# Four bfloat16 sums of halves of x, moved from VectorE to copying and adding transfers

## The chip, the cores and the metric

The kernel runs on one core of a Trainium2 chip. The metric is the device time of one execution in microseconds (us); the time of the kernel before is the median of three runs. The engines are named as the profile names them: PE (TensorE's matmuls) and PEld (its weight loads), DVE (VectorE), ACT (ScalarE), POOL (GpSimd) and SP (SyncE, which here only issues transfers).

## The reference

Two linear-attention blocks, A and B, take the same x of 2048 rows and 640 columns with weights of their own, and a gate mixes their outputs. Everything is bfloat16 outside; there are 32 heads of 20 columns.

```python
qkv = (x @ wqkv) split into q, k, v of 32 heads
phi = lambda t: jnp.where(t > 0, t + 1, jnp.exp(t)) + 1e-6
pq, pk = phi(q), phi(k)
kv = jnp.einsum("bhsd,bhse->bhde", pk, v)
z = jnp.einsum("bhsd->bhd", pk)
o = einsum(pq, kv) / (einsum(pq, z)[..., None] + 1e-6)
block = o.reshape(B, S, D) @ wo
...
g = _sigmoid((x * gate_w).sum(-1, keepdims=True))
return g * a + (1 - g) * b
```

## The kernel before

The kernel never forms v. It computes G = x^T phi(k), a 640 x 640 matrix, for each block, and takes the heads' kv from G and the weights of v afterwards. The 2048 rows of x lie in `xn` as 16 chunks of 128 rows (partitions) with 640 columns each; `xT` holds x transposed; `pk` holds phi(k) like `xn`, `pqT` holds phi(q) transposed.

**Order of the work.** PE's order is written out by hand, and the order of the calls is the order of every engine's instructions. First come the transposes of x and the k chunks of block A (`k_first`, `k_chunk`), with parts of its q. Then the loads of the rest of `xn` (L810), of `wv` and of `wo` (`load_w`, `load_wo`) are issued on SP. In the second part, from L819 on, the last two k chunks of A follow, then `q_pass` (the rest of q of A, L778 to L796), then `g_pass` (column block 4 of G, L447) and `g_strassen` (column blocks 0 to 3 of G, L493). Block B follows with the same two functions after a stage in which its q and k are woven together. At the end come the products with the output weights.

**The product that the change touches.** `g_strassen` computes column blocks 0 to 3 of G with seven block products instead of eight (a Strassen scheme in Winograd's form). x is cut into x11 and x21 (chunks 0 to 7; columns 0 to 255 and 256 to 511) and x12 and x22 (chunks 8 to 15, the same columns). phi(k) is cut into b11 and b12 (chunks 0 to 7; left and right 320 columns) and b21 and b22 (chunks 8 to 15). The scheme needs four sums of halves of x, made once and used by both blocks:

- S1 = x21 + x22 and S2 = S1 - x11, in the tile `S3` (shown as S in the profile)
- S3 = x11 - x21, written over x21 in `xn`
- S4 = x12 - S2, in the first part of the tile `M[1]` (shown as MB in the profile)

Beside them stand four differences of halves of phi(k) for each block: T1 = b12 - b11, T2 = b22 - T1, T3 = b22 - b12, T4 = b21 - T2 (`k_sum`, L474). They lie in `pqT[1]` (pqTB) for block A and in `xT` and a weight tile for block B.

The four sums of x are made by `x_sum` (L464), which issues one DVE instruction each through the helper `add_rows` (L627 is the line that the profile shows). S1 and S2 are called inside the loop at L784, S3 inside the loop at L788, and S4 inside `g_strassen` at L524, behind the fourth difference of phi(k).

PE goes through the products of `g_strassen` in this order: x11 by b11 into the bank `even`; ACT copies that into the bank `odd` (L510). Then S2 by T2 is added into `odd`, x12 by b21 into `even`, S3 by T3 into `odd`, S1 by T1 into a fresh `even`, x22 by T4 into `odd`, S4 by b22 into `even`. DVE combines results with copies u2 and u3 of the banks (L505 through the helper `add`, and L543), ACT copies the others into G (`GT`). Between the products PE also makes the sums for the denominators (`rec_pass`, denA, with DVE's reciprocals at L617 and L622) and spreads the reciprocals (`norm_spread`, exA, L664).

**Queues.** SP issues, in this order around the change: the transposing loads of `xT`, the loads of `xn` (L810), `wvA` (L767), `woA` in two pieces (L773, L774), then `wkB` (which waits until the last k chunk of A has been computed), `g_rows` and `ge` (the gate's row, written to memory and read back spread out, L226 and L229; DVE reads `ge` at L617), and `wqB`. GpSimd issues no transfer in the whole kernel; it makes constants in the first 10 us.

Of the kernel before, what the change touches and what calls it, by code (L numbers as in the profile page):

```python
# [12 lines left out]
ALU = mybir.AluOpType  # L13
# [8 lines left out]
HF = D // 2  # L22
# [10 lines left out]
def kernel(  # L33
# [11 lines left out]
    nc = tc.nc  # L45
# [35 lines left out]
    def ps(name, slot=None):  # L81

        return ps_raw(name, slot).bitcast(FP32).rearrange("p (b n) -> p b n", b=2)
# [27 lines left out]
    SX = {k: S3[:, k - 1] for k in (1, 2)}  # L111
# [47 lines left out]
    for n in range(1, NB):  # L159
        for c in range(DT):  # L160
            nc.sync.dma_start_transpose(
                out=xT[:, c, n * HB:(n + 1) * HB], in_=x2[n * HB:(n + 1) * HB, c * P:(c + 1) * P]
# [4 lines left out]
    for r in range(4):  # L167
# [3 lines left out]
        out=spread[:].rearrange("p (h t) -> p h t", t=TW), in_=I4[:, :, None].to_broadcast([P, H, TW])  # L171
    )
    nc.gpsimd.memset(maskE[:], 1.0)
    for sign, base in ((1, 0), (-1, Dh - 1)):
        nc.gpsimd.affine_select(
            out=maskE[:], in_=maskE[:], pattern=[[-sign * Dh, K6 // Dh], [0, Dh]],
# [3 lines left out]
    for r in range(4):  # L180
        rows = slice(32 * r, 32 * r + 32)
        for sign, base in ((1, 0), (-1, Dh - 1)):
            nc.gpsimd.affine_select(
                out=E4[rows], in_=E4[rows], pattern=[[sign, D]],
# [155 lines left out]
    def q_unit(b, m, h, lifted=False, slot=None, between=None):  # L340

        pt = ps(f"q{'AB'[b]}", slot)
        q_two(b, [(m, 2 * h), (m, 2 * h + 1)], pt)
        phi(pqT[b][:, m, h * 2 * HB:(h + 1) * 2 * HB].rearrange("p (b n) -> p b n", b=2), pt, lifted, between)
# [116 lines left out]
            start=(i == 0), stop=(i == ST - 1),  # L461
        )

    def x_sum(k):  # L464

        x11, x21 = [xn[:, 0:hc, n:n + ic] for n in (0, ic)]
        x12, x22 = [xn[:, hc:ST, n:n + ic] for n in (0, ic)]
        a, b, op = {
            1: (x21, x22, ALU.add), 2: (SX[1], x11, ALU.subtract),
            3: (x11, x21, ALU.subtract), 4: (x12, SX[2], ALU.subtract),  # L470
        }[k]
        add_rows(SX[k], a, b, op)

    def k_sum(b, k):  # L474

        b11, b12 = [pk[:, 0:hc, n * HF:(n + 1) * HF] for n in range(2)]
        b21, b22 = [pk[:, hc:ST, n * HF:(n + 1) * HF] for n in range(2)]
        t = TK[b]
        left, right = {1: lambda: (b12, b11), 2: lambda: (b22, t[1]), 3: lambda: (b22, b12), 4: lambda: (b21, t[2])}[k]()
        add_rows(t[k], left, right, ALU.subtract)  # L480

    def g_prod(pt, left, right, first, between=None):

        for i in range(hc):
            if between is not None and i == hc // 2:
                between()
            for n in range(2):
                nc.tensor.matmul(  # L488
                    pt[:, n, 0:HF], lhsT=left[:, i, n * P:(n + 1) * P], rhs=right[:, i, :],
                    start=(first and i == 0), stop=(i == hc - 1), skip_group_check=not first,  # L490
                )

    def g_strassen(b, select, second, spare):  # L493

        x11, x12 = [xn[:, k:k + hc, 0:ic] for k in (0, hc)]
        x22 = xn[:, hc:ST, ic:2 * ic]
        b11 = pk[:, 0:hc, 0:HF]
        b21, b22 = [pk[:, hc:ST, n * HF:(n + 1) * HF] for n in range(2)]
        lo, hi = GT

        def temp(name):
            return work.tile([P, 2, HF], FP32, tag="osb", name=name, bufs=3)

        def add(dst, pt, sb):
            nc.vector.tensor_tensor(out=dst, in0=pt[:, :, 0:HF], in1=sb[:], op=ALU.add)  # L505

        even, odd = ps("gs0", 0), ps("gs1", second)
        sel = []
        g_prod(even, x11, b11, True, lambda: sel.append(select()))
        nc.scalar.copy(out=odd[:, :, 0:HF], in_=even[:, :, 0:HF])  # L510
        if b == 1:
            for rows in part[1:4]:
                p_diff(rows)
        rts = rec_pass(b, sel[0], 2)
        g_prod(odd, SX[2], TK[b][2], False)
        u2 = temp("u2")
        nc.scalar.copy(out=u2[:], in_=odd[:, :, 0:HF])
        if b == 1:
            k_sum(1, 4)
        g_prod(even, x12, b21, False)  # L520
        nc.scalar.copy(out=lo[:, 0:2, :], in_=even[:, :, 0:HF])
        if b == 0:
            k_sum(0, 4)
            x_sum(4)  # L524
        norm_spread(b, rts, (2, spare))
        g_prod(odd, SX[3], TK[b][3], False)
        u3 = temp("u3")
        nc.scalar.copy(out=u3[:], in_=odd[:, :, 0:HF])
        if b == 1:
            add_rows(TM[0][:], M[0][:, :, HF:D], M[0][:, :, 0:HF], ALU.subtract)  # L530
        scale(b, 0)
        scale(b, 1)
        even = ps("gs0", 0)
        g_prod(even, SX[1], TK[b][1], True)
        add(hi[:, 2:4, :], even, u3)
        scale(b, 2)
        scale(b, 3)
        g_prod(odd, x22, TK[b][4], False)
        nc.scalar.copy(out=lo[:, 2:4, :], in_=odd[:, :, 0:HF])
        scale(b, 4)  # L540
        g_prod(even, SX[4], b22, False)
        for n in range(2):
            nc.vector.tensor_tensor(out=hi[:, n, :], in0=even[:, n, 0:HF], in1=u2[:, n], op=ALU.add)  # L543

    def z_rows(b, slot=None):

# [61 lines left out]
    def rec_pass(b, zsel, slot):  # L608

        pt = ps(f"den{'AB'[b]}", slot)  # L610
        for h in range(2):
            by_group(pt[:, 0, h * RB:(h + 1) * RB], zsel, pqT[b], h)
        rts = []
        for h in range(2):
            part = slice(h * RB, (h + 1) * RB)
            d1 = work.tile([P, RB], FP32, tag="d1", name="d1")
            nc.vector.scalar_tensor_tensor(  # L617
                out=d1[:], in0=pt[:, 0, part], scalar=EPS, in1=ge[:, b, part], op0=ALU.add, op1=ALU.mult
            )
            rT = work.tile([P, RB], BF16, tag="rT", name="rT")  # L620
            with nc.allow_low_precision(reason="a fp32 reciprocal, stored as the bf16 that multiplies bf16"):
                nc.vector.reciprocal(out=rT[:], in_=d1[:])  # L622
            rts.append(rT)
        return rts

    def add_rows(dst, a, b, op):
        nc.vector.tensor_tensor(out=dst, in0=a, in1=b, op=op)  # L627

    def p_diff(rows):

        up = slice(SH + rows.start, SH + rows.stop)
        add_rows(D3[:, :, rows], pqT[0][:, :, rows], pqT[0][:, :, up], ALU.subtract)
# [25 lines left out]
    def norm_spread(b, rts, slots):  # L658

        pts = [ps(f"ex{'AB'[b]}", s) for s in slots]  # L660
        for h in range(2):
            for j in range(4):
                rows = slice(32 * j, 32 * j + 32)
                nc.tensor.matmul(  # L664
                    pts[j // 2][:, j % 2, h * RB:(h + 1) * RB], lhsT=spread[rows, :], rhs=rts[h][rows, :],
                    start=True, stop=True,
                )
        for jj in range(2):
            nc.scalar.copy(
                out=R[:, :, 2 * jj:2 * jj + 2, :].rearrange("p h j n -> p j h n"),  # L670
                in_=pts[jj][:].rearrange("p j (h n) -> p j h n", n=RB),
            )

    def scale(b, m):

        rec = R[:].rearrange("p h j n -> p (h j n)")
        nc.vector.tensor_tensor(out=pqT[b][:, m, :], in0=pqT[b][:, m, :], in1=rec, op=ALU.mult)
# [92 lines left out]
    def load_wo(b, eng):  # L770
        wo_sb[b] = wpool.tile([P, NG, D], BF16, tag="wo", name=f"wo{'AB'[b]}")
        if b == 0:
            eng.dma_start(out=wo_sb[0][:K6, 0:DT], in_=wo_dram[0][0:DT * K6].rearrange("(j p) f -> p j f", p=K6))  # L773
            eng.dma_start(out=wo_sb[0][:D - DT * K6, DT], in_=wo_dram[0][DT * K6:D])  # L774
            return
        eng.dma_start(out=wo_sb[b][:KG], in_=wo_dram[b].rearrange("(j p) f -> p j f", p=KG))

    def q_pass(units):  # L778

        units = list(units)  # L780
        q_unit(0, *units.pop(0))
        zr = z_rows(0)
        gate_spread()
        for k in range(2):  # L784
            x_sum(1 + k)
            q_unit(0, *units.pop(0), True)
        zsel = z_pass(0, zr)
        for k, (m, h) in enumerate(units):  # L788
            if k < 2:
                if k:  # L790
                    x_sum(3)
                else:
                    k_sum(0, 2)
            q_unit(0, m, h, True)
        sq_sum(4, 0)
        return zsel  # L796
# [12 lines left out]
    for n in range(1, NB):  # L809
        nc.sync.dma_start(  # L810
            out=xn[:, n * CB:(n + 1) * CB, :], in_=x2[n * HB:(n + 1) * HB, :].rearrange("(q p) d -> p q d", p=P)
        )
    wv[0] = load_w(0, "v", nc.sync)
    load_wo(0, nc.sync)

    def bank(pool, name, n=1):
        return pool.tile([P, HB] if n == 1 else [P, n, HB], FP32, tag=name, name=name)

    with tc.manual_schedule():  # L819
# [120 lines left out]
        t = wpool.tile([P, 2, DT, HF], BF16, tag="wq", name="TM12")  # L940
# [101 lines left out]
```

## Time and profile before

| what | value |
|---|---|
| median of three runs | 189.27 us (188.78 to 189.38) |
| the profiled execution's own time | 189.34 us |
| its span in the profile | 187.6 us |
| busy PE, PEld | 182.6 us (97%), 122.5 us (65%) |
| busy DVE, ACT, POOL | 155.8 us (83%), 87.0 us (46%), 9.1 us (5%) |
| granted clock of TensorE | 1.0 |
| moved by transfers | 16.18 MB, a mean of 86 GB/s |

The profile is of one execution, and its times count from the start of the span. The span covers what the profile records of the engines; the execution's own time is 1.74 us longer. A row of a group gives the line, the engine, the operation, output and inputs, the shapes and the count; then the total busy time, the mean of one in ns, and the idle time of the engine just before them. Issuing a transfer is not counted as busy time, so SP and a GpSimd that only issues show none. A busy PE is not yet a PE at its peak, since the ends of its matmuls are modelled: the rows show 299 ns for one of 320 columns, while 16 of them follow each other in 2.17 us, 136 ns apart.

### The profile page before, as it was taken

How to read it: one execution, taken by the hardware profiler on the slowest of the kernel's cores; microseconds unless marked ns; L12 is line 12 of the kernel's file. 1: busy time of each engine (PE TensorE's matmuls, PEld its weight loads, DVE VectorE, ACT ScalarE, POOL GpSimd, SP SyncE). 2: the span in 40 equal slices, each digit the busy share in tenths (PEclk: the TensorE clock that was granted, in tenths of full speed). 3: DMA queues.
4: the chain of work that ended last, by engine and by line, in shares of the span. 5: the costliest groups of instructions: out<-in, count | busy, mean ns of one | idle time of the engine just before them, and what ended most of it. 6: DMA issues, size and time to landing. Idle time of an engine off the chain costs nothing.

```text
span 187.6 us, 3635 instructions
## 1 busy us (share of the span) xinstructions
PE 182.6 (97%) x1447; PEld 122.5 (65%) x1456; DVE 155.8 (83%) x268; ACT 87.0 (46%) x150; POOL 9.1 (5%) x25
## 2 busy tenths in 40 slices
PE   8899999999999999999999999999999999999993
PEld 3666657765577677676666655767677776777772
DVE  1468868889999999998898987999997989787554
ACT  2065488545842432455868686662611611111110
POOL 8920000000000000000000000000000000000000
PEclk9999999999999999999999999999999999999999
DMA  5996449984250000005000000145600003312222
GB/s 181 277 171 86 101 98 302 349 205 152 56 178 0 0 3 0 0 3 175 0 0 5 0 0 0 34 141 198 159 0 0 3 0 104 109 70 71 73 72 70
DMA packets 19769, 16.18 MB, mean 86 GB/s; under 512 B 8968, under 2 KB 19624, under 8 KB 19752
## 3 DMA queue, kind: packets, MB, share of 16 engines
q1 hardware_dynamic: 18888, 15.13, 29.3%
q10 hardware_dynamic: 864, 0.82, 1.3%
q8 instruction: 11, 0.18, 0.4%
q14 instruction: 6, 0.05, 0.1%
HBM read 10.52 MB, written 3.46 MB: 74 GB/s over the span
## 4 chain that ended last, share of the span: by engine, by line
PE 90%; DMA 4%; DVE 3%; issue 1%; ACT 1%; DVEq 0%; ACTq 0%
PE gs L488 17%; PE qA L329 11%; PE kB L277 11%; PE kA L277 10%; PE q L383 7%; PE ox L688 6%; PE oy L688 5%; PE oz L688 5%; DMA wkA<-in_A_wqkv_dram 3%; PE ow L688 3%; PE gB L459 2%; PE gA L459 2%; DMA xn<-in_A_x_dram 2%; PE qB L329 1%; PE q L329 1%; DVE osb L693 1%
## 5 line engine op out<-in xcount | busy, mean ns | idle before, releaser
L277 PEld LDWEIGHTS <-xT 128*128 128x128 bf16 x320 | 31.0, 97 | 15.2 <-issue 1.0
L256 DVE TENSOR_SCALAR e<-e 128x640 bf16<-128x640 bf16 (+2 forms) x56 | 19.4, 346 | 7.9 <-ACT e L251 7.4
L277 PE MATMUL kB<-wkB,xT 128*128 128x320 bf16 x160 | 24.2, 299 | 0.0
L277 PE MATMUL kA<-wkA,xT 128*128 128x320 bf16 (+1 forms) x160 | 23.0, 299 | 0.5 <-ACT wkA L212 0.3
L329 PE MATMUL qA<-xT,wqA 128*128 128x512 bf16 x96 | 22.4, 379 | 0.2
L329 PEld LDWEIGHTS <-wqA 128*128 128x128 bf16 x100 | 11.7, 118 | 9.2 <-issue 0.3
L251 ACT ACTIVATE e<-kA 128x640 bf16<-128x640 f32 x16 | 11.2, 706 | 10.1 <-PE kA L277 10.0
L488 PEld LDWEIGHTS <-xn 128*128 128x128 bf16 x128 | 12.2, 98 | 5.1 <-issue 0.3
L251 ACT ACTIVATE e<-kB 128x640 bf16<-128x640 f32 x16 | 11.3, 708 | 9.0 <-PE kB L277 8.9
L265 DVE SCALAR_TENSOR_TENSOR pk<-kA,e 128x640 bf16<-128x640 f32 x16 | 13.2, 825 | 2.1
L265 DVE SCALAR_TENSOR_TENSOR pk<-kB,e 128x640 bf16<-128x640 f32 x16 | 13.2, 824 | 1.5
L251 ACT ACTIVATE e<-qA 128x1024 bf16<-128x1024 f32 x10 | 10.2, 1023 | 8.2 <-PE qA L329 7.9
L732 ACT COPY u<-ox 128x320 f32<-128x320 f32 x8 | 3.4, 425 | 21.6 <-PE ox L688 21.6
L251 ACT ACTIVATE e<-q 128x512 bf16<-128x512 f32 x18 | 10.8, 597 | 5.4 <-PE q L383 3.8
L688 PEld LDWEIGHTS <-xT 128*128 128x128 bf16 x85 | 8.0, 98 | 3.1 <-DVE xT L627 0.2
L688 PEld LDWEIGHTS <-pqTA 128*128 128x128 bf16 x85 | 7.9, 98 | 2.9 <-issue 0.2
L688 PEld LDWEIGHTS <-pqTB 128*128 128x128 bf16 x80 | 7.8, 98 | 3.0
L693 DVE TENSOR_TENSOR osb<-oz,u 128x320 bf16<-128x320 f32 (+1 forms) x18 | 8.0, 453 | 2.0 <-PE oz L688 0.9
L383 PE MATMUL q<-xT,wqB 128*128 128x512 bf16 x32 | 9.5, 379 | 0.0
L488 PE MATMUL gs<-pk,xn 128*128 128x320 bf16 x64 | 9.5, 299 | 0.0
L459 PEld LDWEIGHTS <-xn 128*128 128x128 bf16 x64 | 6.3, 98 | 3.0 <-issue 0.4
L716 ACT COPY p1s<-ox 128x320 f32<-128x320 f32 x8 | 3.4, 425 | 10.3 <-PE ox L688 10.3
(150 smaller groups left out, 319.2 us busy)
## 6 DMA issues: line engine op xcount, KB each, us to landing
out_dram<-osb SPq DMA_DIRECT2D x14, 160.0 KB, 1.9
xn<-in_A_x_dram SPq DMA_DIRECT2D x3, 640.0 KB, 5.7
wvA<-in_A_wqkv_dram SPq DMA_DIRECT2D x1, 800.0 KB
wkB<-in_B_wqkv_dram SPq DMA_DIRECT2D x1, 800.0 KB, 4.8
wqB<-in_B_wqkv_dram SPq DMA_DIRECT2D x1, 800.0 KB, 4.8
wvB<-in_B_wqkv_dram SPq DMA_DIRECT2D x1, 800.0 KB
MA<-m_rows SPq DMA_DIRECT2D x1, 800.0 KB, 4.5
woB<-in_B_wo_dram SPq DMA_DIRECT2D x1, 800.0 KB
```

What stands on the lines that cost most here:

```text
L251: nc.scalar.activation(out=to, in_=part, func=ACT.Exp)
L256: nc.vector.tensor_scalar(self.e, self.e, 1.0, EPS, op0=ALU.min, op1=ALU.add)
L265: nc.vector.scalar_tensor_tensor(out=dst, in0=src, scalar=1.0 + EPS, in1=e, op0=ALU.add, op1=ALU.max)
L277: nc.tensor.matmul(pt[:, hf, 0:n], lhsT=xT[:, c, i * P:(i + 1) * P], rhs=wk[b][:, c, hf * HF:hf * HF + n], start=(c == 0), stop=(c == DT - 1),
L329: nc.tensor.matmul(dst, lhsT=mixed(wq[b][:, c, :], m), rhs=xT[:, c, n * HB:(n + 1) * HB], start=first, stop=last,)
L383: nc.tensor.matmul(dst, lhsT=left(c), rhs=right(c), start=first and k == 0, stop=k == len(cs) - 1, skip_group_check=not first,)
L459: nc.tensor.matmul(pt[:, hf, 0:HF], lhsT=xn[:, i, c * P:(c + 1) * P], rhs=pk[:, i, hf * HF:(hf + 1) * HF], start=(i == 0), stop=(i == ST - 1),
L488: nc.tensor.matmul(pt[:, n, 0:HF], lhsT=left[:, i, n * P:(n + 1) * P], rhs=right[:, i, :], start=(first and i == 0), stop=(i == hc - 1), s ...
L688: nc.tensor.matmul(dst, lhsT=left[:, c, r0:r0 + P], rhs=right[:, c, :], start=(first and c == 0), stop=(c == DT - 1), skip_group_check=not ...
L693: nc.vector.tensor_tensor(out=dst, in0=acc, in1=sb, op=ALU.add)
L716: nc.scalar.copy(out=self.p1s[:], in_=self.at("x"))
L732: nc.scalar.copy(out=self.u2[:], in_=self.at("x"))
```

## The change

`x_sum` becomes `x_sums`, called once, right behind the load of `wo` and before the second part of the work. It issues seven transfers of 128 x 2048 values. Three on SP copy x21 to S1, x11 to S2 and x12 to S4. Four on GpSimd's queue add in the transfer: x22 to S1, S1 to S2, x11 to x21 (which becomes S3 in place), and S2 to S4. A transfer can add but not subtract, so the second column block of x is taken with its sign turned: the sums are now x21 + x22, x11 + S1, x21 + x11 and x12 + S2. To match, two of the differences of phi(k) are turned (b11 - b12 and b12 - b22), T2 becomes b22 + T1, the copy from `even` to `odd` becomes a multiplication by -1 on ACT, and the two additions of u2 and u3 on DVE become subtractions.

```diff
-    def x_sum(k):
+    def x_sums():
 
         x11, x21 = [xn[:, 0:hc, n:n + ic] for n in (0, ic)]
         x12, x22 = [xn[:, hc:ST, n:n + ic] for n in (0, ic)]
-        a, b, op = {
-            1: (x21, x22, ALU.add), 2: (SX[1], x11, ALU.subtract),
-            3: (x11, x21, ALU.subtract), 4: (x12, SX[2], ALU.subtract),
-        }[k]
-        add_rows(SX[k], a, b, op)
+        for k, a in ((1, x21), (2, x11), (4, x12)):
+            nc.sync.dma_start(out=SX[k], in_=a)
+        for k, b in ((1, x22), (2, SX[1]), (3, x11), (4, SX[2])):
+            nc.gpsimd.dma_start(out=SX[k], in_=b, accum_op=ALU.add)
...
-        left, right = {1: lambda: (b12, b11), 2: lambda: (b22, t[1]), 3: lambda: (b22, b12), 4: lambda: (b21, t[2])}[k]()
-        add_rows(t[k], left, right, ALU.subtract)
+        left, right = {1: lambda: (b11, b12), 2: lambda: (b22, t[1]), 3: lambda: (b12, b22), 4: lambda: (b21, t[2])}[k]()
+        add_rows(t[k], left, right, ALU.add if k == 2 else ALU.subtract)
...
-        def add(dst, pt, sb):
-            nc.vector.tensor_tensor(out=dst, in0=pt[:, :, 0:HF], in1=sb[:], op=ALU.add)
-
...
-        nc.scalar.copy(out=odd[:, :, 0:HF], in_=even[:, :, 0:HF])
+        nc.scalar.mul(out=odd[:, :, 0:HF], in_=even[:, :, 0:HF], mul=-1.0)
...
             k_sum(0, 4)
-            x_sum(4)
...
-        add(hi[:, 2:4, :], even, u3)
+        nc.vector.tensor_tensor(out=hi[:, 2:4, :], in0=u3[:], in1=even[:, :, 0:HF], op=ALU.subtract)
...
-            nc.vector.tensor_tensor(out=hi[:, n, :], in0=even[:, n, 0:HF], in1=u2[:, n], op=ALU.add)
+            nc.vector.tensor_tensor(out=hi[:, n, :], in0=even[:, n, 0:HF], in1=u2[:, n], op=ALU.subtract)
...
         for k in range(2):
-            x_sum(1 + k)
             q_unit(0, *units.pop(0), True)
         zsel = z_pass(0, zr)
         for k, (m, h) in enumerate(units):
-            if k < 2:
-                if k:
-                    x_sum(3)
-                else:
-                    k_sum(0, 2)
+            if k == 0:
+                k_sum(0, 2)
             q_unit(0, m, h, True)
...
     load_wo(0, nc.sync)
+    x_sums()
```

## The prediction

> **What bounds the kernel now.** The page comes first: its busy line, and four of the rows of its 40 slices (4.7 us each).
>
> ```profile
> PE 182.6 (97%) x1447; PEld 122.5 (65%) x1456; DVE 155.8 (83%) x268; ACT 87.0 (46%) x150; POOL 9.1 (5%) x25
> ...
> PE   8899999999999999999999999999999999999993
> ...
> DVE  1468868889999999998898987999997989787554
> ...
> POOL 8920000000000000000000000000000000000000
> ...
> DMA  5996449984250000005000000145600003312222
> ```
>
> PE works in every slice but the ends. DVE is nearly as full from slice 9 to 15, where the four sums stand, and GpSimd has nothing to do after the third slice. Two full engines side by side call for the stage view, here the stretches from 42 to 73 us (columns: length, busy PE, PEld, DVE, ACT, POOL, granted clock, DMA share, GB/s).
>
> ```profile
> 42.00:52.00 10.00, 9.92 (x68) 5.45 (x62) 9.69 (x13) 6.93 (x9) 0.00 (x0) 1.00 0.35 106
> 52.00:60.00 8.00, 8.00 (x91) 5.72 (x90) 7.76 (x12) 3.35 (x5) 0.00 (x0) 1.00 0.35 104
> 60.00:73.00 13.00, 13.00 (x102) 9.14 (x101) 12.72 (x12) 4.60 (x6) 0.00 (x0) 1.00 0.00 1
> ```
>
> PE is idle for 0.08 us of these 31, DVE for 0.83. So the question is which waits for which. The chain of work that ended last answers it:
>
> ```profile
> 51.86 4.35 PE gA L459 x32
> 56.20 2.17 PE gs L488 x16
> 58.38 1.21 PE denA L203 x40
> 59.58 4.45 PE gs L488 x32
> 64.03 0.33 PE exA L664 x8
> 64.36 8.80 PE gs L488 x64
> 73.16 2.72 PE kB L277 x20
> ```
>
> Every piece is PE and each begins where the last ends. The view of PE's waits from 39 to 187 us is empty, too. Adding up the holes between matmuls in the trace from 39 to 182 us gives 0.52 us in nine holes, none of them behind a DVE sum (seven are 0.05 us each). So PE bounds the stage, and DVE, though 97% busy, is never what PE waits for.
>
> **What the change removes.** Four rows of DVE, one for each sum:
>
> ```profile
> L627 DVE TENSOR_TENSOR xn<-xn 128x2048 bf16<-128x2048 bf16 x1 | 1.2, 1220 | 0.0
> L627 DVE TENSOR_TENSOR S<-S,xn 128x2048 bf16<-128x2048 bf16 x1 | 1.2, 1219 | 0.0
> L627 DVE TENSOR_TENSOR S<-xn 128x2048 bf16<-128x2048 bf16 x1 | 1.2, 1216 | 0.0
> L627 DVE TENSOR_TENSOR MB<-xn,S 128x2048 bf16<-128x2048 bf16 x1 | 1.2, 1212 | 0.0
> ```
>
> 1220 + 1219 + 1216 + 1212 ns = 4.87 us less DVE work between 45.6 and 66.5 us. Its worth is what PE waited for it: nothing. The most that could come back is the 0.52 us of holes in all. I take 0.
>
> **What only changes its form.** k_sum keeps its four instructions and its shapes; two swap their operands and one adds instead of subtracting (rows of 1.43 to 1.49 us either way): 0. At L535 and L543 an add of PSUM and SBUF becomes a subtract: 0. The copy of the first product into the second bank (L510, ACT, 0.68 us at 58.46) becomes a multiplication by -1. ACT ends it at 59.14 and PE uses it at 59.51, so there are 0.37 us of room; ACT's Identity with a bias takes 1108 ns where Exp takes 1023 for 1024 columns, so a form may cost 0.1 us, less than the room. From below, 0: a copy that ended earlier would release nothing. I take 0 both times, A and B.
>
> **What it adds: seven transfers, and the wait of PE for them.** Each moves 128 x 2048 bf16 = 524 KB. Their due times are PE's first reads (PE rows; S is S1 or S2, MB holds S4):
>
> ```profile
> 59.51 2.35 PE L488 MATMUL gs<-pqTB,S 128*128 128x320 bf16 x16
> ...
> 64.30 2.35 PE L488 MATMUL gs<-pqTB,xn 128*128 128x320 bf16 x16
> 66.48 2.34 PE L488 MATMUL gs<-pqTB,S 128*128 128x320 bf16 x16
> ...
> 70.83 2.34 PE L488 MATMUL gs<-pk,MB 128*128 128x320 bf16 x16
> ```
>
> So S2 is due at 59.5, S3 at 64.3, S1 at 66.4, S4 at 70.7. Before a late sum PE stands still, since its order is fixed, and everything behind it moves by as much.
>
> *The copies.* They queue on SP behind woA:
>
> ```profile
> 29.84 1.08 SPq L773 DMA_DIRECT2D woA<-in_A_wo_dram  x1
> 30.96 2.47 SPq L774 DMA_DIRECT2D woA<-in_A_wo_dram  x1
> 39.35 0.39 SPq L767 DMA_DIRECT2D wkB<-in_B_wqkv_dram  x1
> 43.16 0.33 SPq L226 DMA_DIRECT2D g_rows<-gr  x1
> 44.59 1.76 SPq L229 DMA_DIRECT2D ge<-g_rows  x4
> 51.89 0.39 SPq L767 DMA_DIRECT2D wqB<-in_B_wqkv_dram  x1
> ```
>
> SP is free at 33.4. Issuing three takes 1.5 us by the xn loads' 0.5 each, or 7.4 by the slowest row, so wkB leaves at 39.35 or 1.5 later. In the table of issues woA lands 11.8 us after it is issued, at 41.6, and the copies' packets stand behind its own. A copy is 1024 pieces of 512 B, 64 for each of 16 engines; the trace's 512 B packets take 27 ns, so 1.73 us each. S1's copy ends at 43.3; with 0.7 us (half of the 1.4 us that the 16 KB g_rows takes from issue to landing) it is known at 44.0. The three push what is queued behind them by 5.2 us: wkB lands at 49.4 instead of 44.2 (due at 73), ge at about 54 instead of 49 (DVE reads it at 59.73), wqB hardly (due at 74). All are covered, ge by the least, some 5 us.
>
> *The adds.* GpSimd's queue takes them in order: S1 += x22, S2 += S1 (waits for the first to land), S3 += x11, S4 += S2 (waits for the second). What waits behind a waiting add is only the next add. No transfer of GpSimd and no add stands in this trace, so each part gets two ends:
> - Data: one pass at best (1.73 us). At worst I count two, since both operands are read: 3.5 us for the first and third (512 B pieces). For the second and fourth both sides lie in one run of 4 KB for a partition: 1280 B packets take 55 ns and 6400 B ones 244, so about 160 ns for 4 KB, 8 per engine, twice: 2.6 us. I take two passes.
> - Start and landing: 1.4 us, from g_rows.
> - Describing the pieces: r ns for each of 1024, 128, 1024 and 128. SP's 640-piece rows give 0.39 to 1.27 us, 0.6 to 2.0 ns a piece. GpSimd does it in software; its own rows take 0.71 us for 640 elements, 1.1 ns a step, so eight steps a piece would be 9 ns. Between 0.6 and 9 I take 2.6, just above SP's slowest, the nearest row of the same kind of work.
>
> S2 then lands at 44.0 + (1.4 + 3.5 + 1.024r) + (1.4 + 2.6 + 0.128r) = 52.9 + 1.15r: 55.9 with r = 2.6, 3.6 us early. S3 is described once the second add has been, so it lands at 48.9 + 1.15r + 1.024r + 4.9 = 53.8 + 2.18r = 59.5, 4.8 us early. S4 follows S2 by 4.0 + 0.3: 60.2, or 63 behind S3, over 7 us early. Sharing engines with ge and wqB (2.2 us of packets each at most) still leaves all of them early. Cost: 0.
>
> DVE's TENSOR_SCALAR and CAST rows from 44 to 59.5 sum to 2.0 us (0.42 x 4 and 0.32). If GpSimd can't describe pieces beside them, S2 comes at 57.9 and is still early; if every DVE row blocks it, rival 1 has the price. The Trainium skill, SBUF — State Buffer, section "A bandwidth-pool intuition that's wrong (but worth ruling out)" and the box above it, speaks against the change here: a transfer issued from GpSimd starves while DVE runs in a two-port mode, since its descriptors can't be written meanwhile, and one of 0.62 us took 3.1 so. No run here has shown that yet.
>
> **The sum** against the profiled execution (189.34, its span 187.6 and 1.74 around it; the median of the runs is 189.27, lower by 0.07): 189.34 - 0 + 0 = 189.3.
>
> **Rivals.**
> 1. *The adds are late* (slower). It decides at r = 4.8 ns, where S3 reaches 64.3; S2 joins at 5.7. Take r = 7: S2 at 61.0, late by 1.5; S3 at 69.0, due at 65.8 by then, late by 3.2 more; S4 in time. 189.3 + 4.7 = 194.0. The far end is a GpSimd that every DVE row blocks (DVE leaves it 0.3 us in 10 from 42 to 52): the adds then wait until PE's stop empties DVE near 64, and S2, a whole 12 us of chain later, is some 16 us late: 205. For it: GpSimd's slow rows, a chain of two transfers, DVE at 97%. Against it: data of 2.6 to 3.5 us against 15.5 us of room, and DVE's own share falls by 4.9 us.
>
>    The clock is 1.00 in every stage row. The Trainium skill, TensorE: Matmul & The Clock Gate, section "What's actually happening", says the clock is halved after about 3.4 us without work; a stall of 4.7 us could by that cost a window more, 1.7 us, about 195.7.
> 2. *DVE's freedom is worth something* (not slower; faster). It would have to show as fewer holes in PE: at most 0.52 us, 188.8. Against it: seven holes are 0.05 us each and end with nothing that DVE does.
> 3. *A queue not used before costs time at the ends*, in setting up or draining. Nothing in the profile speaks for it; 1.74 us lie around the span now, and as much again would be 191.1.
>
> **Chances.** About 0.6 us is 0.3% here, near what a measurement can tell from no change. Adds hidden, 189.3: 0.50. Adds late: 0.38, of which 0.30 around 194.0 and 0.08 for the far end, 205. Ends: 0.05. DVE's gain: 0.07, of which 0.05 pass the bound if more hides in it than I see. So faster 0.05, same 0.52, slower 0.43. The hidden case alone spans 188.8 to 189.8. The range goes up into the late case, to 195.0, and leaves out its far part, some 0.14, and 0.04 below 188.6.
>
> **What would show it.** Right: DVE has four rows fewer, PE's gs rows still begin at 59.5, 64.3, 66.5 and 70.8, and SP's copies are issued before wkB. Wrong: a hole of PE ahead of the S or xn product whose releaser is a DMA; GpSimd's four issue rows then say whether r (rows of over 5 us) or the data (short rows, late landings) was mis-sized. A late ge would show as DVE waiting at L617.

## The result and the profile after

| | before | after |
|---|---|---|
| median of 20 runs | 189.14 us (188.74 to 189.75) | 190.37 us (189.38 to 191.71) |
| the profiled execution, its span | 189.34, 187.6 us | 190.97, 189.2 us |

The ratio is 1.0065 [1.0047, 1.0084]: slower by 1.23 us, inside the forecast range (188.6 to 195.0), but not the likeliest case (189.3). The changed kernel also scatters more, over 2.3 us instead of 1.0. The figures of e2 and e3 below leave out their slow runs (three of six and one of six, 194 to 197 us).

The page after the change, its busy line and four rows of slices (4.7 us each):

```profile
PE 182.9 (97%) x1447; PEld 122.6 (65%) x1456; DVE 151.7 (80%) x264; ACT 87.0 (46%) x150; POOL 14.3 (8%) x29
...
PE   7999999999997999999999999999999999999993
...
DVE  1478868887785979998897987999997989787554
...
POOL 8910000006011000000000000000000000000000
...
DMA  6997459999998500005000000045700002312222
```

DVE has its four rows and 4.1 us of work less. PE has as much work as before, but the thirteenth slice (56.8 to 61.5 us) falls from 9 to 7. GpSimd shows work in slices 10, 12 and 13: other than SP's issues, its rows for the adds count as busy (14.3 us against 9.1). The transfers are busy from slice 7 to slice 13 without a break. The page's list of queues has the adds as a software queue: 2.10 MB take 7.7% of the 16 engines' span where the largest hardware queue's 16.70 MB take 32.4%, so a byte that is added takes about 1.9 times as long (7.7/2.10 against 32.4/16.70).

The stage view of the same stretches (length, busy PE, PEld, DVE, ACT, POOL, clock, DMA share, GB/s):

```profile
42.00:52.00 10.00, 9.93 (x68) 5.49 (x58) 7.71 (x11) 6.93 (x9) 3.43 (x2) 1.00 1.20 244
52.00:60.00 8.00, 7.52 (x87) 5.28 (x84) 6.35 (x10) 3.30 (x5) 0.87 (x1) 1.00 1.13 234
```

DVE is freed as intended (9.69 to 7.71 us in the first stretch), yet PE falls from 8.00 to 7.52 us in the second. The DMA share went from 0.35 to 1.20 and 1.13: over one, so packets of several queues stand in the engines at once. PE's waits from 39 to 187 us, a view that was empty before (us in total, times, longest):

```profile
PE gs L487 <- DMA S<-S: 1.3, 1, 1.3
PE q L383 <- DVE q L401: 0.2, 1, 0.2
```

The first is the rival's mark: PE stands before a product that reads S, and a DMA ends the wait. The chain of waits says which (start, length, what), and GpSimd's timeline shows the four adds:

```profile
52.04 8.69 DMA S<-S
60.73 0.05 issue
60.77 4.52 PE gs L487 x32
```

```profile
44.11 1.70 POOL L471 DMA_DIRECT2D S<-xn  x1 [33.66 <-DMA S<-xn]
45.15 2.39 POOL L471 DMA_DIRECT2D xn<-xn  x1
52.04 0.87 POOL L471 DMA_DIRECT2D S<-S  x1 [4.50 <-DMA S<-xn]
61.01 0.85 POOL L471 DMA_DIRECT2D MB<-S  x1 [8.10 <-DMA S<-S]
```

S2's add (S<-S) waits for S1's, is issued at 52.04 and lands at 60.73, 8.7 us later. PE wants it at 59.52 and starts at 60.77. A transfer lands in 16 parts, one for each DMA engine: 15 of S2's had landed by 59.62, and PE waited the rest for the last one. Besides, the adds do not run in the order of the code: S3's (xn<-xn) is issued at 45.15, ahead of S2's. So, other than the description of the kernel says, the order of the calls is not that of every engine's instructions: GpSimd's order is the scheduler's where the code does not fix it, and S2's add had to wait. Landings by the trace: S1 51.76, S3 56.04, S2 60.73, S4 65.46.

The shift of PE against before is 1.25 us from the first S product on, 1.33 from exA on (0.08 more, behind DVE's row with `ge`), and 1.7 from 105.0 on, where the second wait of 0.2 us stands. The profiled execution is 1.63 us longer than its partner. DVE's row with `ge`, before and after:

```profile
59.73 0.42 DVE L617 SCALAR_TENSOR_TENSOR d<-denA,ge 128x256 f32<-128x256 f32 x1
```

```profile
61.09 0.42 DVE L612 SCALAR_TENSOR_TENSOR d<-denA,ge 128x256 f32<-128x256 f32 x1 [1.97 <-issue]
```

The view names no releaser, but the last part of `ge` lands at 60.91. So there is a second path, as late as the first: the row starts 1.36 us later than before, and the second half of exA, which needs the reciprocals behind it, 1.34 us later (65.42 against 64.08).

### The profile page after: what moved, and what is told of

Its sections match the earlier page's. It is cut to its first block, busy times and chain, and to the rows that moved or that the text cites. A ratio compares the mean times of both kernels' runs of the same rounds, so it can differ in the third digit from the quotient of the medians.

```text
span 189.2 us, 3647 instructions
## 1 busy us (share of the span) xinstructions
PE 182.9 (97%) x1447; PEld 122.6 (65%) x1456; DVE 151.7 (80%) x264; ACT 87.0 (46%) x150; POOL 14.3 (8%) x29
## 3 DMA queue, kind: packets, MB, share of 16 engines
q1 hardware_dynamic: 22008, 16.70, 32.4%
## 4 chain that ended last, share of the span: by engine, by line
PE 62%; SPq 11%; DMA 11%; issue 10%; DVE 3%; ACT 1%; ACTq 0%; POOL 0%; POOLq 0%; DVEq 0%
PE gs L487 15%; SPq L161 10%; PE kB L277 10%; PE q L383 7%; DMA xn<-in_A_x_dram 6%; PE ox L683 6%; PE oy L683 5%; PE oz L683 5%; DMA S<-S 5%; PE ow L683 3%; PE gB L459 2%; PE qB L329 1%; PE q L329 1%; DVE osb L688 1%; PE mA L894 1%
## 5 line engine op out<-in xcount | busy, mean ns | idle before, releaser
L487 PEld LDWEIGHTS <-S 128*128 128x128 bf16 x64 | 6.1, 98 | 4.0 <-DMA S<-S 1.5
```

The source lines that it names most:

```text
L487: nc.tensor.matmul(pt[:, n, 0:HF], lhsT=left[:, i, n * P:(n + 1) * P], rhs=right[:, i, :], start=(first and i == 0), stop=(i == hc - 1), s ...
```

## The experiments

The theory: S2's add is late because of the traffic it shares engines with, and two things are candidates: S3's add, ahead of it in GpSimd's queue, and the loads on SP, `wqB` above all, issued at 53.4. The rival at the start: PE has a second late path, the chain from `ge` (landed at 60.9, before at 49.3) over DVE's row at L612 to exA, which would show as soon as S2 came in time. Each measurement below is a median against that of the kernel before, and then the measured ratio with its 95% interval. The ratio is not the quotient of the two medians and can differ from it by 0.1%, in e2 by 0.3%.

**e1: the adds in the order of the code.** S1, S2, S3, S4.

```diff
-    x_sums()
+    with tc.manual_schedule():
+        x_sums()
```

> GpSimd's adds in the order S1, S2, S3, S4; in the changed kernel S3's add went ahead of S2's. Theory of two late paths (S2 late because S3's packets stand ahead of it in GpSimd's queue, and ge late by as much, unseen behind it): S2 is issued near 52, lands near 57 instead of 60.7, so PE has no hole at its first S product (59.5); but ge still lands near 61, so PE stands still some 1.4 us ahead of exA, and the time stays near 190.3. Rival (S2 is the only late path): no hole at either place, 189.1. Rival (S2 is late because of the engines it shares with ge and wqB, not because of the order): S2 still lands after 59.5 and the hole stays where it was, 190.3.

Measured: 190.08 us against 189.15; 1.0047 [1.0026, 1.0069]. GpSimd's rows for the adds of S2 and S3, the row of S2's add in the list of issues (KB, us to landing) and PE's wait in e1:

```profile
51.91 1.07 POOL L471 DMA_DIRECT2D S<-S  x1 [6.48 <-DMA S<-xn]
52.51 2.06 POOL L471 DMA_DIRECT2D xn<-xn  x1
```

```profile
S<-S POOLq DMA_DIRECT2D x1, 512.0 KB, 8.3
```

```profile
PE gs L487 <- DMA S<-S: 1.1, 1, 1.1
```

With nothing of GpSimd's ahead of it, S2's add still takes 8.3 us. Its first packet moves only at 55.1, 3.2 us after its issue, when 463 of the 640 packets of `wqB` (issued on SP at 51.4) have started. `ge` lands at 53.6 here and DVE's L612 row starts in time, at 59.16, so the second path is gone and the wait for S2 is not. Order alone is not the cure.

**e2 and e3: `wkB` issued behind `ge`,** so that `ge` comes early; e3 with the order of e1 as well.

```diff
-    wk[1] = load_w(1, "k", nc.sync)
     k_sum(0, 1)
...
+    wk[1] = load_w(1, "k", nc.sync)
     wq[1] = load_w(1, "q", nc.sync)
```

> The load of wkB is issued behind ge instead of ahead of g_rows, so the gate's rows no longer queue behind it. Theory of two late paths: ge lands by 52, DVE's first L612 instruction starts at 59.7 as in the kernel before, but S2 still lands at 60.7 or later (wkB and wqB now both share the engines with its add), so the hole of 1.25 us or more at the first S product stays: 190.3 to 191.5. Rival (ge alone is the cause): no hole, 189.1.

> Both edits together: the adds in order and wkB behind ge. Theory of two late paths: S2 lands by 58.5 and ge by 52, no hole of PE from 52 to 74 us, 189.1 to 189.3, as before the change. Rival (sharing the engines decides): S2's packets, now beside wkB and wqB, land near 60 or later, and a hole of 0.5 us or more stays, 189.7 or more.

Measured, against 189.15: e2 190.43 us, 1.0097 [1.006, 1.0134]; e3 190.25 us, 1.0067 [1.0046, 1.0088]. In both PE waits 0.8 us for S2 (landed 60.31 and 59.79), with `ge` in time (DVE's row at 59.6 in e2). In e3 S3, now behind S2's add and beside `wkB` and `wqB`, takes 14.2 us from issue to landing, is late too and costs 0.28 us. Here moving a load only chose which transfer is late. With `ge` in time the wait for S2 stays, so `ge` is not the cause of that wait; what a late `ge` would cost without it, these two runs do not show.

**e4: the same traffic, but nobody waits for it.** The seven transfers are made with the same shapes; S1 and S2 are also made by DVE, as additions, and PE reads those. The transfers that would make S1 and S2 write to tiles that nobody reads at that time; S3 and S4 still come from transfers.

```diff
+    SY = {1: flat(M[0], "p c d -> p (c d)", ic), 2: flat(R, "p h j n -> p (h j n)", ic), 3: SX[3], 4: SX[4]}
...
+        for k, a in ((1, xn[:, 0:hc, ic:2 * ic]), (2, xn[:, 0:hc, 0:ic]), (4, xn[:, hc:ST, 0:ic])):
+            nc.sync.dma_start(out=SY[k], in_=a)
+        nc.gpsimd.dma_start(out=SY[1], in_=xn[:, hc:ST, ic:2 * ic], accum_op=ALU.add)
...
+        nc.gpsimd.dma_start(out=SY[k], in_={2: SY[1], 3: xn[:, 0:hc, 0:ic], 4: SX[2]}[k], accum_op=ALU.add)
...
+            x_sum(1 + k)
+            if k == 0:
+                x_add(3)
+            else:
+                x_add(2)
+                x_add(4)
             q_unit(0, *units.pop(0), True)
```

> The same seven transfers of the same sizes, but S1 and S2 are also made by DVE and PE reads those; the first two copies and adds go to tiles that nobody reads before they are written again. So PE waits for no S1 or S2 from a transfer, and only their traffic is left. Theory of two late paths: no hole at the first S product, ge lands near 61 all the same, DVE's first L612-like instruction (d from denA and ge) starts near 61 instead of 59.7, and PE stands still 1.3 us ahead of exA: 190.3. Rival (S2 is the only late path): no hole, 189.1.

Measured: 189.25 us against 189.15; 1.0009 [0.9988, 1.003]. PE's waits from 39 to 187 us are empty again, though the transfer in S2's place lands at 60.6, as late as S2 in the changed kernel:

```profile
42.00:52.00 10.00, 9.93 (x68) 5.47 (x58) 9.69 (x13) 6.93 (x9) 3.23 (x2) 1.00 1.23 272
52.00:60.00 8.00, 8.00 (x91) 5.73 (x90) 6.88 (x11) 3.34 (x5) 1.75 (x2) 1.00 1.17 231
```

So the traffic in itself costs PE nothing (DMA share 1.23 and 1.17, PE 8.00 of 8.00): the price is the wait for what it delivers. I had expected a hole at exA from a late `ge` and there is none; but `ge` landed at 57.99, in time for DVE, so that this run does not test a `ge` as late as in the changed kernel.

**e5 and e6: `wqB` issued some 10 us later,** by ACT, behind its copy to u2; e5 with the order of the changed kernel, e6 with that of e1.

```diff
+        if b == 0:
+            wq[1] = load_w(1, "q", nc.scalar)
...
-    wq[1] = load_w(1, "q", nc.sync)
```

> The changed kernel with the load of wqB issued by ACT behind its copy of u2 (near 62 us) instead of by SP near 53, so that S2's add shares the engines with ge alone; the adds keep their order. Theory after the first four runs (S2's add costs 4.5 us alone and 8 to 8.7 us here, of which about 2 us are S3's packets ahead of it and the rest engines shared with SP's loads): S2 lands between 59 and 60 instead of at 60.7, the hole at the first S product shrinks from 1.25 us to below 0.8, and the time to 189.3 to 189.9. Rival (the order alone): the hole stays at 1.2 us, 190.3.

> Both things that the theory blames are taken from S2's add: the adds run in the order S1, S2, S3, S4, and wqB is loaded from near 62 us on. Theory: S2 takes about as long from issue to landing as S4's add does alone (4.5 us), lands by 57.5, PE has no hole at the first S product and none at S3's; 189.1 to 189.3. Rival (a transfer that adds is slow while DVE works, whoever shares the engines): S2 still takes 8 us, lands near 60, the hole of about 1 us stays, 190.1.

Measured: e5 190.53 us against 189.10, 1.0062 [1.0041, 1.0083]; e6 189.50 against 189.10, 1.0011 [0.9999, 1.0024]. The issue rows that differ, first of e5, then of e6:

```profile
S<-S POOLq DMA_DIRECT2D x1, 512.0 KB, 8.9
```

```profile
S<-S POOLq DMA_DIRECT2D x1, 512.0 KB, 5.1
```

In e5 PE's wait stays 1.2 us, against my expectation of less than 0.8: S3's add ahead, and `ge`, are enough to hold S2 up. (In the changed kernel the packets of `wqB` start only at 58.2, when most of S2's have moved.) In e6 S2 lands at 56.86, PE's S product starts at 59.71 right behind denA, and no wait for a DMA is left. Each of the two, S3's add ahead and `wqB` beside, is sufficient, and only taking both away helps. From the changed kernel (1.0065) to e6 that is 0.54%, some 1.0 us. But `ge` is in time in e6 as well (landed 53.54, in e5 60.67), so what e6 takes away is both late paths, S2's and `ge`'s.

**e7: the sums left out.** No transfers, no sums; the products read x's halves in their places. This tells what is left of the difference when the sums cost nothing at all.

```diff
-    SX = {k: S3[:, k - 1] for k in (1, 2)}
+    SX = {1: xn[:, 0:hc, ic:2 * ic], 2: xn[:, 0:hc, 0:ic]}
...
-    SX[4] = flat(M[1], "p c d -> p (c d)", ic)
+    SX[4] = xn[:, hc:ST, 0:ic]
...
-    x_sums()
```

> Leaves the four sums of x out: neither DVE nor a transfer makes them, and the products read the halves x21, x11, x21 and x12 in their place. So DVE is 4.87 us freer than before the change and no transfer is added; this is the most that the change could bring. Theory (PE bounds the stage and waits for no DVE sum): the same as before, 189.0 to 189.2. Rival (DVE's freedom is worth something): below 188.6.

Measured: 189.65 us against 189.10; 1.0026 [1.0013, 1.0039]. Without any sum the kernel is slower than before, not faster. PE's only wait is the second one of the changed kernel (0.2 us for DVE's q), and the DVE row ahead of that one's has a pause of its own:

```profile
102.11 0.82 DVE L264 SCALAR_TENSOR_TENSOR pk<-kB,e 128x640 bf16<-128x640 f32 x1 [0.47 <-PE q L382]
```

The same row in before:

```profile
101.80 0.83 DVE L265 SCALAR_TENSOR_TENSOR pk<-kB,e 128x640 bf16<-128x640 f32 x1
```

DVE stands still for 0.47 us, where it went on in before, some 30 us after the last product that reads a sum in this block, in a kernel with none of the transfers. The product of q that the view names as the releaser need not be one: in e11, below, the same row starts at 102.01, before that product ends (102.31).

**e8: the turned signs alone,** with the sums on DVE as additions where they were before.

```diff
+        a, b = {1: (x21, x22), 2: (SX[1], x11), 3: (x11, x21), 4: (x12, SX[2])}[k]
+        add_rows(SX[k], a, b, ALU.add)
...
```

> The turned signs alone: ACT's multiplication by -1, the swapped differences of phi(k) and the two subtractions, with the four sums made by DVE where they stood before, as additions. Theory: each edit costs nothing, 189.1 to 189.2, and the row of the multiplication is the 0.68 us of the copy. Rival (the form costs time on ACT's or DVE's way to PE): 189.5 or more, with a hole ahead of the first S product though no transfer is there.

Measured: 189.44 us; 1.0005 [0.999, 1.002], with no wait of PE. The turned signs cost nothing that can be measured; the multiplication's row has 688 ns against the copy's 677.

**e9 and e10: the transfers earlier.** e9 issues `x_sums` ahead of `wvA` and `woA`; e10 moves those two loads behind `wqB` as well.

```diff
+    x_sums()
     wv[0] = load_w(0, "v", nc.sync)
     load_wo(0, nc.sync)
-    x_sums()
```

> The changed kernel with the seven transfers issued ahead of the loads of wvA and woA, right behind the loads of xn; nothing else moves. Theory (S2 is late only by what shares its queue and engines): the copies no longer wait for woA, S1's add is issued near 37 instead of 44, S2 lands by 52, so no hole at the first S product even with S3 ahead in the queue; what is left is the small hole of 0.19 us near 104: 189.3 to 189.6. Rival (the start doesn't matter, the adds just take longer beside wvA and woA, 1.55 MB more to share with): S2 lands after 59.5, 190.0 or more.

> As the run before, and the loads of wvA and woA go behind that of wqB, near 53 us (wvA is first read near 83, woA near 119), so that the adds share the engines with wkB and ge alone. Theory: S2 lands by 50, ge by 52, no hole before 100; 189.3 to 189.6, as e6, with the 0.19 us near 104 left. Rival (wvA comes too late): a hole ahead of the masks' products near 83.

Measured: e9 190.82 us, 1.0101 [1.0076, 1.0126]; e10 189.78, 1.0035 [1.0023, 1.0048]. In e9 S1's add is issued 6.5 us earlier (37.57) and lands only 0.6 us earlier (51.15), with `wvA`, `woA` and `wkB` beside it. S2 lands at 58.39, in time in the profile, but a new hole opens. PE's wait in e9, and then two DVE rows, which take 0.33 us each in before:

```profile
PE qA L329 <- DVE pqTA L265: 0.5, 1, 0.5
```

```profile
38.85 0.79 DVE L256 TENSOR_SCALAR e<-e 128x640 bf16<-128x640 bf16 x1
...
40.52 0.48 DVE L256 TENSOR_SCALAR e<-e 128x640 bf16<-128x640 bf16 x1
```

They run while GpSimd describes the pieces of S1's and S3's adds (37.57 to 40.85). Against its times in before, DVE is 0.18 us late ahead of them and 0.63 us late behind them. Neither theory nor rival had this; the 1.0101 is also more than the profile's holes explain, so part of it is open. In e10 S2 lands at 52.79, 6.6 us early, and the hole from DVE is 0.17 us. What is left in its profile is that and the hole near 104, 0.37 us together; the time is above the 189.3 to 189.6 expected, and the rest of the 0.35% is open.

**e11 and e12: DVE's count restored.** The hole near 104 stood in every kernel with 264 DVE instructions and in none with 266 or 268. e11 is e6, and e12 is e7 (sums left out), each with more memsets of one small tile on DVE in the set-up, which makes 268 and 269 instructions.

```diff
-    nc.vector.memset(lift[:], 1.0 + EPS)
+    for k in range(5):
+        nc.vector.memset(lift[:], 1.0 + EPS)
```

> The kernel of e6 (adds in order, wqB late) with four DVE instructions more: the tiny memset of 128 x 1 at the start is made five times instead of once. Theory for the hole of 0.19 us near 104, which stands in every kernel with four DVE instructions fewer and in none with all of them: it comes from where DVE's stream of instructions is cut for its fetches, so it goes when the count is again that of the kernel before, though DVE does nothing more in the middle: no hole there, 189.1. Rival (the hole comes from the transfers or from DVE running ahead): it stays, 189.5.

> Leaves the four sums of x out as e7 did, with five tiny memsets more at the start, so that DVE's count is that of the kernel before. Theory (the hole near 104 goes with the count, and PE waits for no DVE sum): no hole there, 189.1, the same as before the change: 4.87 us of DVE's time are worth nothing. Rival (DVE's freedom is worth something, hidden in e7 by the hole): below 188.8. Rival (the hole is not of the count): 189.6 as e7.

Measured: e11 189.06 us against 189.14, 0.9996 [0.9985, 1.0008]; e12 (six memsets) 189.01, 0.9993 [0.9982, 1.0005]. In both the hole is gone: DVE's row (102.01 in e11, 101.45 in e12) starts without a pause.

So more work on DVE took 0.0015 (e6 to e11) and 0.0033 (e7 to e12) off the ratio, 0.3 and 0.6 us. That more instructions at the start remove the hole is shown, in the profiles by both pairs and in the times by e7 and e12, whose intervals do not overlap; those of e6 and e11 do. Why is open. A packet of 8 KB of the instruction queue q14 lies at 102.8 to 104.2 us in the changed kernel, e6 and e7, and at 100.5 to 100.8 in before, e4, e8, e11 and e12, which speaks for a late fetch of instructions. But in the first three it starts 0.7 us after DVE's pause has ended, and the pause ends 0.07 us after that product of q in each of them, which speaks for a wait.

e12 also settles what DVE's time is worth. Its stages without any sum:

```profile
42.00:52.00 10.00, 9.97 (x63) 5.49 (x52) 7.60 (x12) 6.93 (x9) 0.00 (x0) 1.00 0.28 97
52.00:60.00 8.00, 8.00 (x91) 5.69 (x89) 6.85 (x11) 3.03 (x5) 0.00 (x0) 1.00 0.34 104
```

PE has 9.97 and 8.00 us, before 9.92 and 8.00: DVE's 4.87 us are worth 0.05 us of PE here, and nothing measurable in all.

## Why the prediction was right in one part and wrong in another

The time lies inside the range because the range reached up into the late case; the likeliest case, 189.3, was 1.1 us too low.

**Right: PE bounds the stage, and the removal is worth nothing.** e12 bears it out (0.9993 [0.9982, 1.0005]); no kernel of this study is faster than before beyond its interval. Rival 2, DVE's freedom, is not seen; by the interval at most 0.3 us of it could hide. So the change could at best break even.

**Right: the forms.** e8: 1.0005 [0.999, 1.002].

**Right: the copies and the first add.** S1's copy was put at 44.0; S1's add starts at 44.11. The add was to take 1.4 + 3.5 + 1.024 x 2.6 = 7.6 us; it took 7.65 (44.11 to 51.76). That it fits to 0.05 us is luck, for the parts are off both ways: the trace's adding packets of 512 B take 65 ns where plain ones take 27, 2.4 passes instead of 2, and describing takes 1.7 to 1.9 ns a piece instead of 2.6 (GpSimd's row of 1.70 us for 1024 pieces; the first packet follows the issue by 3.2 us for 1024 pieces and 1.4 for 128). Adding packets of 4 KB take 328 ns, where 2 x 160 = 320 were taken.

**Wrong: the order.** The adds were taken to run as S1, S2, S3, S4; they ran as S1, S3, S2, S4.

**Wrong, and the step that failed:** "Sharing engines with ge and wqB (2.2 us of packets each at most) still leaves all of them early. Cost: 0." S2's add was to take 4.3 us (1.4 + 2.6 + 0.3). Nearly alone, as S4's add of the same size shows, it does: 4.5 us (61.01 to 65.46). In e6, in order and without `wqB`, it takes 5.1 and lands at 56.9, 1.0 us from the forecast 55.9. In the changed kernel it takes 8.7: S3's packets hold it until about 55.0, it then shares the engines with `ge`, and one engine lands 1.1 us after the 15 others (59.62 to 60.73). The slack of 3.6 us was counted against the packets' own time; a queue behind others costs its wait for them, too. In e1 `wqB`, counted with 2.2 us of packets, kept the first packet 3.2 us from the issue, where S4's came after 1.4.

The last engine had most of the price. In e2, e3 and e5 15 of the 16 parts of S2 had landed even before PE wanted it (59.15, 58.95 and 58.87 against 59.56, 59.04 and 59.30), and the last part alone made the hole. In these three and in the changed kernel the trace has a packet of 16 KB of another instruction queue, q8, that starts at 55.3 to 56.5 us and takes 0.9 to 1.3 us. That it held up the one engine fits the size of the delay, but is not shown: the packets of the trace do not name their engine.

**Wrong: ge's cover.** It was to land at about 54, some 5 us early. It landed at 60.9: `g_rows`, which it waits for, landed at 49.14 instead of 44.57, its four issues took 4.13 us instead of 1.76, and from the start of the last one to its landing 8.9 us passed instead of 3.4. DVE waited 2.0 us at L612. That stood beneath the hole of S2 but for 0.08 us, so here it cost next to nothing on top. It is not harmless, though: with S2 in time, this `ge` would still have held the second half of exA by some 1.3 us (an estimate from its start, 65.42 against 64.08). No run has S2 in time and `ge` so late; in e6 both are in time.

**Rival 1 came true, smaller and by another mechanism.** It was the right place, the right mark (a releasing DMA ahead of an S product) and the right side. But it was to be decided by r, GpSimd's time for a piece, and GpSimd's rows are short (1.70 us for 1024 pieces, 0.87 for 128): the data's wait in the engines decided. Its price was 4.7 us at r = 7; it was 1.25 us in the profile, and 1.0 us from the changed kernel to e6, with `ge`'s path. S3, forecast as its larger part, was early, having gone ahead. The far end, a GpSimd that busy DVE locks out, did not occur: in e4 DVE has 9.69 of 10 us, as before, and GpSimd's row for S1's add is 1.70 us there too. The starved descriptors of the Trainium skill, SBUF — State Buffer ("A bandwidth-pool intuition that's wrong (but worth ruling out)"), were not seen in the adds. The clock stayed at 1.00 through the stall of 1.25 us; the Trainium skill, TensorE: Matmul & The Clock Gate, section "What's actually happening", puts the loss at about 3.4 us without work, which no profile here reached.

**Rival 3, the ends, was not seen.** The profiled execution is 1.77 us longer than its span, before 1.74.

**Not foreseen: the small hole near 104.** It belongs to the removal, whose worth was put at 0: four DVE instructions fewer cost 0.2 to 0.35 us by the shift of PE in the profiles, 0.3 and 0.6 us by the ratios. The 1.0 us that e6 takes away and this 0.3 make up about the 1.23 us.

Not tried: taking `ge`'s packets away from S2 alone, S2 in time with `ge` late, and what part of e1's 8.3 us is the plain load's share.

## What to carry to other kernels

Time that an engine is freed of is worth what the bounding engine waited for it, and here a run with the sums left out showed that to be nothing, so that the transfers could only lose. A chain of transfers has to be costed with everything that is queued on the same engines between its first issue and its last landing, in the order that the scheduler really issues it, and with the slack compared to that wait, to the last of the engines, rather than to the packets' own time. Where two things each suffice to keep a transfer late, undoing either one alone shows no gain, and only the run without both finds the cause.

## What the runs showed of the hardware

- A transfer that adds costs more per packet than one that copies: 65 against 27 ns at 512 B.
- A transfer lands with the last of its 16 engines: of S2's add in the changed kernel 15 had landed by 59.62 us and the last at 60.73.
- The packets of GpSimd's queue can stand behind those of SP's. In e1 the add was issued at 51.91 and its first packet moved at 55.14, with `wqB` under way; in e6, without `wqB` beside it, it was issued at 51.81, moved at 53.26 and had landed at 56.86.
- SP's issues took longer in the changed kernel than before: 4.13 against 1.76 us for the four of `ge`, 0.93 against 0.33 for `g_rows`, 1.57 against 0.39 for `wkB`. What lengthens them is open: that of `wkB` ends before the first add is issued, and in e1 and e6 the four of `ge` take 1.76 and 1.79 us beside S1's add.
- While GpSimd described pieces, some TENSOR_SCALAR rows of DVE took longer: 0.79 and 0.48 us instead of 0.33 in e9, 0.74 instead of 0.43 in e6. None did in the changed kernel, and GpSimd's row for S1's add was 1.70 us in all three. The Trainium skill, SBUF — State Buffer, section "Who interferes with whom", calls the port pair that the two share an exclusive lock; the trace agrees in so far as DVE was held up in e9 and e6.
- DVE paused 0.46 to 0.48 us in all kernels with 264 DVE instructions, at the same row, and in none with 266 to 269.
